# PSUM copies by lateness, dk in 16 B runs, small outputs as rows, K flips on TensorE: a change to a convolution-and-gated-unit gradient kernel

## The chip, the core and the metric

The kernel runs on one core of one Trainium2 chip. The core has five engines with in-order instruction streams of their own: TensorE (PE in the profile, its weight loads PEld), VectorE (DVE), ScalarE (ACT), GpSimd (POOL) and SyncE (SP). Here SP only issues DMAs, and POOL issues most of the others. TensorE writes its results to PSUM, eight banks of 2 KB in each of 128 partitions; VectorE and ScalarE carry them from there to SBUF. The metric is device time in microseconds for one execution that computes all outputs.

## The reference

The forward function takes q, k, v (2048 tokens, 512 channels, bf16) and weights, and the kernel returns its value and nine gradients.

```python
xn = layernorm(q)
k_shift = sum(k shifted by t, t = 0..3, times shift_k[:, t])
kv = k_shift * v
y = irfft(rfft(kv padded) * rfft(ssm_k padded))[:S] + kv * ssm_D
g = silu((sigmoid(xn @ w_gate) * (xn @ w_up)) @ w_down)
out = q + (xn * y) * g
# returned: out, and the gradients of q, k, v, shift_k, ssm_k, ssm_D,
#           w_gate, w_up, w_down for a given grad_out
```

So out_0 is the value, out_1 to out_3 the gradients of q, k and v, out_4 (512 x 4) that of shift_k, out_5 (512 x 2048) that of ssm_k, called dk in the code, out_6 (512) that of ssm_D, and out_7 to out_9 those of the weights.

## The kernel before

**How it is recorded and ordered.** The program isn't written in the order in which it runs. Generators ("streams") call operations on a recorder, `Rec`, which notes each one with its reads and writes. `run_streams` interleaves the streams: each has a weight and a start and end fraction, and the stream that is furthest behind is advanced. That gives every operation a number. At the end `Rec.order` plays all operations through a simple model of the five engines (`cost` for compute, `dcost` for DMAs, whose transfers go through one modelled pipe) and always takes the operation that can start first; equal starts go to the lower number. A PSUM tile gets its banks at that point too, of the kind that it asks for (`mm2`: three pairs of banks; `mm2c`, used in the last stage: two pairs; `acc`: two banks; `tr`: two banks). `emit` then issues the operations in that order, so each engine's in-order stream is fixed by the model's idea of time. All instructions have one source line in the profile, L467, for that reason, and are told apart by engine, operation, shape and place in time.

**Copies out of PSUM.** `evac` (L229) records an operation with two alternatives, a ScalarE copy and a VectorE copy. Before the change both engines have it in their queues of ready work, and the one that can start first takes it. A DMA is held back until it would start at most 8 us ahead of the end of the modelled pipe (L418).

**The stages.** The channels are worked in four column groups of 128 (`cg`).

1. First stage, up to about 160 us. `strK` transposes ssm_k and takes it through `step1` (matmuls with the table Cf) and a flip, a 128 x 128 transposition of blocks from Qg to Qf; `strV` forms kv on VectorE (eight tensor-tensor operations of 2048 elements a group) and does the same; `strX` does `step3`, the complex product `cmul` on VectorE, `inv3` and `inv1`, which leave y. Spectra go to DRAM (KK_d). Beside them `strG` runs the gate and up projections of eight token blocks. V's flips are transposes on TensorE with a PSUM copy (`flip`, L805); K's are two DMA transposes of SBUF (`flip_dma`, L814), issued by SP.
2. The token stage, `stepB`, up to about 395 us: sixteen token blocks through the gated unit and back (z, d, x). Transposed copies of its activations go out through DMA transposes on SP (`token_major`), and are read again as L blocks (`ld_L`) for the weight gradients.
3. The last stage. `frontC` and `backC` take the gradient of y back through the same transform, with KK loaded from DRAM, and `dW` (35 output blocks of 16 matmuls, accumulated in `acc` banks) fills TensorE between them. For each column group `backC` loads vg, ksh and kh (`ld_bwd`, called at L1185 ahead of step3), does four quarters (`qq`) of step3, two products and two inv3, then inv1, forms dks with VectorE and two small SBUF-to-SBUF DMAs for the rows that cross partitions, then makes dk: two PSUM tiles of 16 matmuls with Ci, each copied to dKT (L1225). dKT has the 16 values j of one n side by side, and the copy walks over j outside and n inside. Then follow the diagonal of shift_k (one `tr` bank), seven tensor-tensor operations for the gradient of k, and the stores.

**The end.** After the last group `backC` reorders the diagonals into skout and stores out_4 from it (L1257), and out_6 from dDo (L1258), by SP, both from a layout with channels on partitions: out_4 in pieces of four values, out_6 in pieces of one.

Of the kernel before, what the change touches and what calls it, by code (L numbers as in the profile page):

```python
# [166 lines left out]
class Rec:  # L167
# [141 lines left out]
    def dcost(self, alt):  # L309

        eng, meth, a, k = alt
        dst, src = a[0], a[1]
        nb = math.prod(dst.shape) * esize(dst.dtype)
        if "transpose" in meth:
            return nb / 176e3 + 0.3, nb / 176e3
        run = 1 << 20
        for v in (dst, src):
            dims = [d for d in v.ap if d[1] > 1]
            r = 1
            for s, n in reversed(dims if str(v.space) == "DRAM" else [d for d in v.ap[1:] if d[1] > 1]):  # L320
                if s != r:
                    break
                r *= n
            run = min(run, r * esize(v.dtype))
        rate = 320e3 if run >= 2048 else 280e3 if run >= 1024 else 220e3 if run >= 512 else 120e3 if run >= 256 else run * 400
        par = dst.shape[0] if str(dst.space) != "DRAM" else src.shape[0]
        d = nb / rate
        if par < 16:
            d = min(d * 16, d + 1.0)
        return (0.56 if eng == "gpsimd" else 0.45), d  # L330

    def order(self):
# [23 lines left out]
        now = {e: [] for e in self.ENGS}  # L356
        banks = [0.0] * 8
# [6 lines left out]
        def push(op):  # L364
            for q, alt in enumerate(op.alts):
                heapq.heappush(soon[alt[0]], (op.ready, op.n, q))
# [13 lines left out]
        while ndone < len(ops):  # L380
            best = None
            for e in self.ENGS:
                while soon[e] and (soon[e][0][0] <= free[e] or ops[soon[e][0][1]].done):
                    r, n, q = heapq.heappop(soon[e])
                    if not ops[n].done:
                        heapq.heappush(now[e], (n, q))
                while now[e] and ops[now[e][0][0]].done:
                    heapq.heappop(now[e])
                if now[e]:
                    c = (free[e], now[e][0][0], e, now[e][0][1], True)  # L390
                elif soon[e]:
                    c = (soon[e][0][0], soon[e][0][1], e, soon[e][0][2], False)
                else:
                    continue
                if best is None or c[:2] < best[:2]:
                    best = c
            if best is None:
                raise RuntimeError("the order is stuck: " + str({k: len(v) for k, v in blocked.items()}))
            t, n, e, q, isnow = best
            heapq.heappop(now[e] if isnow else soon[e])  # L400
            op = ops[n]
            new = [v for v in op.tiles if v.bank is None]
# [12 lines left out]
            alt = op.alts[q]  # L415
            if op.dma:
                occ, d = self.dcost(alt)
                t = max(t, pipe - 8.0)  # L418
# [12 lines left out]
            seq.append((op, q, t))  # L431
# [29 lines left out]
    def emit(self):  # L461
        seq = self.order()
        place = lambda v: v.place() if isinstance(v, PT) else v
        with self.tc.manual_schedule(), self.nc.allow_non_contiguous_dma(reason="tiny"):
            for op, q, _ in seq:
# [94 lines left out]
def kernel_impl(ctx, tc, A_q, A_k, A_v, A_shift_k, A_ssm_k, A_ssm_D, B_x, B_w_gate, B_w_up, B_w_down,  # L560
# [296 lines left out]
    def strK():  # L857
        for cg in range(NG):
# [16 lines left out]
            flip_dma(Qg, Qf)  # L875
            yield 1
# [65 lines left out]
    run_streams([(gG, len(FA) * 11776, 0.1, 0.97), (strK(), 4 * 6144, 0.0, 0.7), (strV(), 4 * 16384, 0.0, 0.8),  # L942
# [236 lines left out]
    def backC():  # L1179
        for cg in range(NG):  # L1180
# [4 lines left out]
            ld_bwd(cg)  # L1185
# [4 lines left out]
            for qq in range(5):  # L1190
                if qq < 4:
# [9 lines left out]
                    ys[qq] = (Y1, Y2)  # L1201
                if qq > 0:
# [16 lines left out]
            for jh in range(2):  # L1219
# [5 lines left out]
                nc.evac(dKT[:, :, 8 * jh:8 * jh + 8].rearrange("p n j -> p j n"), pk[:], 1024)  # L1225
# [31 lines left out]
        nc.sync.dma_start(out_4.rearrange("(db p) t -> p db t", p=P), skout)  # L1257
        nc.sync.dma_start(out_6.rearrange("(cg p) -> p cg", p=P), dDo)  # L1258
# [15 lines left out]
    for r in [wdT_r, wgT_r, wuT_r, sig_r, h_r, xq2_r, go_r, dg_r, du_r, wq_r, dh_r,  # L1274
# [17 lines left out]
    term_r = Ring(ar, [NJ, GW])  # L1292
    dm = ar.view(term_r.blks[0][0], [4, 128], f32)
# [4 lines left out]
                        (gated(backC(), "back"), 4 * 38912 + 4096, -0.05, 0.72)], until=lambda: "back" in flags)  # L1298
# [66 lines left out]
```

## Time and profile before

| what | value |
|---|---|
| median of 3 runs | 658.59 us (657.49 to 660.03) |
| the profiled execution | 659.44 us |
| its span, first to last instruction | 657.7 us |
| mean granted TensorE clock | 0.942 |
| DMA, mean over the span | 198 GB/s |
| DMA packets under 512 B | 126311 of 178163 |

The profile shows one execution. The busy time of an engine is the time in which it executes; idle time before an instruction is put down to what it waited for last. In the table by stretches each row gives a stretch, its length and the busy time of PE, PEld, DVE, ACT and POOL with instruction counts, then the granted clock, the mean busy share of the DMA engines and GB/s. A timeline row gives start, length, engine, operation, what it writes and reads, the count of merged instructions, and in brackets the idle time before it with its cause. A row of a group gives busy time and the mean in ns, then the idle time before. A row of DMA issues gives the count, KB each and the median time from issue to landing. SPq is the sequencer of SP.

### The profile page before, as it was taken

What the parts mean: (1) busy time and instruction counts of PE and PEld (TensorE: products, weight loads), DVE (VectorE), ACT (ScalarE), POOL (GpSimd) and SP (SyncE); (2) the same over time, 40 slices, a digit from 0 to 9 for tenths busy, and PEclk for the clock granted to TensorE, in tenths of its full rate; (3) what the DMA queues carried; (4) which work ended last, traced back from release to release, by engine and by line L of the source; (5) the groups of instructions that cost most, each with busy time, mean ns of one, the idle gap of its engine ahead of it and who ended that gap; (6) DMA issues with size and microseconds to landing.
All of it is one profiled execution on the core that took longest, in us unless ns stands there. A gap on an engine that the chain in (4) does not pass through costs nothing.

```text
span 657.7 us, 12345 instructions
## 1 busy us (share of the span) xinstructions
PE 544.7 (83%) x4940; PEld 365.6 (56%) x4996; DVE 489.5 (74%) x921; ACT 286.3 (44%) x352; POOL 150.5 (23%) x259
## 2 busy tenths in 40 slices
PE   4867888997799698998999895599865988998952
PEld 3756667774567465665666562345643554754531
DVE  7599899976889769898887781138627988778704
ACT  7547688641434233443343350114452472552700
POOL 2215143222112222222211020112112133241111
PEclk9979899998899899999999998879977999899996
DMA  8898985999959857998578999999974759585272
GB/s 252 222 225 239 272 222 195 260 224 194 232 146 232 202 137 204 175 225 236 151 186 218 245 242 139 107 253 175 283 201 125 186 170 310 179 273 160 76 57 80
DMA packets 178163, 130.09 MB, mean 198 GB/s; under 512 B 126311, under 2 KB 158905, under 8 KB 178106
## 3 DMA queue, kind: packets, MB, share of 16 engines
q1 hardware_dynamic: 161162, 75.52, 54.0%
q0 software_dynamic: 16416, 53.78, 29.7%
q8 instruction: 39, 0.64, 0.4%
q14 instruction: 18, 0.15, 0.1%
q10 hardware_dynamic: 528, 0.00, 0.0%
HBM read 52.79 MB, written 46.11 MB: 150 GB/s over the span
## 4 chain that ended last, share of the span: by engine, by line
PE 40%; DVE 31%; issue 10%; DMA 10%; ACT 6%; POOL 2%; POOLq 0%; DVEq 0%; ACTq 0%
PE psum L467 40%; DVE slab L467 31%; DMA slab<-slab 7%; ACT slab L467 6%; DMA slab<-in_A_q_dram 2%; POOL slab L467 1%; DMA slab<-in_grad_out_dram 1%; POOL out_dram L467 1%; DMA out_dram<-slab 1%; DVEq L467 0%; POOL KK_d L467 0%; POOLq L1360 0%; POOLq L467 0%; ACTq L467 0%; POOLq L1349 0%
## 5 line engine op out<-in xcount | busy, mean ns | idle before, releaser
L467 PE MATMUL psum<-slab 128*128 128x128 bf16 (+4 forms) x4940 | 544.7, 271 | 101.5 <-DVE slab L467 47.7
L467 PEld LDWEIGHTS <-slab 128*128 128x128 bf16 (+1 forms) x4996 | 365.6, 101 | 280.2 <-issue 87.7
L467 DVE TENSOR_TENSOR slab<-slab 128x512 bf16<-128x512 bf16 (+5 forms) x551 | 301.8, 587 | 30.3 <-DMA slab<-slab 12.8
L467 ACT CAST slab<-psum 128x1024 bf16<-128x1024 f32 (+2 forms) x188 | 179.4, 994 | 209.9 <-PE psum L467 156.1
L467 DVE CAST slab<-psum 128x1024 bf16<-128x1024 f32 (+2 forms) x67 | 73.7, 1108 | 61.0 <-PE psum L467 47.7
L467 POOL DMA_DIRECT2D out_dram<-slab x75 | 44.1, 592 | 275.5 <-DVE slab L467 197.3
L467 ACT ACTIVATE slab<-psum 128x512 bf16<-128x512 f32 (+1 forms) x64 | 36.5, 574 | 55.8 <-PE psum L467 53.3
L467 DVE TENSOR_TENSOR slab<-psum,slab 128x512 bf16<-128x512 f32 (+2 forms) x68 | 44.0, 653 | 19.0 <-PE psum L467 12.7
L467 ACT ACTIVATE slab<-slab 128x512 bf16<-128x512 bf16 (+3 forms) x51 | 40.1, 797 | 40.2 <-DVE slab L467 39.6
L467 ACT COPY slab<-psum 128x512 bf16<-128x512 bf16 (+1 forms) x46 | 34.2, 757 | 48.5 <-PE psum L467 36.4
L467 POOL DMA_DIRECT2D KK_d<-slab x32 | 19.9, 628 | 55.1 <-DVE slab L467 32.2
L467 DVE SCALAR_TENSOR_TENSOR slab<-slab 128x1 f32<-128x1 f32 (+3 forms) x64 | 28.0, 437 | 3.4 <-ACT slab L467 2.2
L467 POOL DMA_DIRECT2D slab<-in_A_q_dram x29 | 16.1, 556 | 50.1 <-ACT slab L467 31.4
L467 DVE SCALAR_TENSOR_TENSOR slab<-psum,slab 128x512 f32<-128x512 f32 x16 | 11.0, 690 | 18.0 <-PE psum L467 18.0
L467 DVE TENSOR_SCALAR slab<-slab 128x1 f32<-128x1 f32 (+8 forms) x49 | 16.8, 358 | 1.7 <-ACT slab L467 1.0
L467 POOL DMA_DIRECT2D slab<-KK_d x16 | 11.6, 728 | 25.3 <-DVE slab L467 25.3
L467 DVE COPY slab<-psum 128x1024 bf16<-128x1024 bf16 (+1 forms) x18 | 11.2, 627 | 4.4 <-PE psum L467 4.1
L467 POOL TENSOR_TENSOR slab<-slab 128x1 f32<-128x1 f32 (+1 forms) x20 | 12.4, 624 | 8.5 <-DVE slab L467 8.3
L467 DVE BATCH_NORM_STATS2 slab<-slab 128x6 f32<-128x512 bf16 x16 | 11.0, 686 | 2.6 <-DMA slab<-in_A_q_dram 2.6
L467 DVE MEMSET slab<- 32x192 uint32 (+2 forms) x7 | 1.1, 165 | 15.2 <-DMA slab<-slab 14.1
L467 POOL DMA_DIRECT2D slab<-in_grad_out_dram x16 | 8.7, 542 | 12.4 <-DMA out_dram<-slab 12.1
L467 POOL DMA_DIRECT2D slab<-in_A_k_dram x12 | 10.1, 845 | 3.9 <-PE psum L467 2.8
(22 smaller groups left out, 43.3 us busy)
## 6 DMA issues: line engine op xcount, KB each, us to landing
KK_d<-slab POOLq DMA_DIRECT2D x32, 256.0 KB, 4.5
slab<-KK_d POOLq DMA_DIRECT2D x16, 512.0 KB, 5.9
out_dram<-slab POOLq DMA_DIRECT2D x58, 128.0 KB, 3.6
hS_d<-slab SPq DMA_DIRECT2D x16, 352.0 KB, 2.9
dgS_d<-slab SPq DMA_DIRECT2D x16, 352.0 KB, 3.5
duS_d<-slab SPq DMA_DIRECT2D x16, 352.0 KB, 3.3
slab<-hS_d SPq DMA_DIRECT2D x8, 512.0 KB, 6.0
slab<-dgS_d SPq DMA_DIRECT2D x8, 512.0 KB, 12.6
```

The costliest lines, as they stand in the source:

```text
L467: getattr(getattr(self.nc, eng), meth)(*[place(v) for v in a], **{x: place(v) for x, v in k.items()})
```

## The change

Five things change in the code, and none in the arithmetic.

1. `order`: an operation with two alternatives is no longer in both engines' queues. ScalarE takes it when it comes first there. VectorE may take it only when ScalarE would start it late: by over 0.4 us if VectorE has nothing else within 0.6 us, by over 1.6 us otherwise.
2. `dcost`: other prices. DMA transposes occupy SP for less time; POOL's DMAs with runs of 256 B or more are priced like runs of 1 KB; other rates are higher; a DMA may now start 9 us ahead of the pipe's end.
3. K flips: `flip` on TensorE instead of `flip_dma`; the weight of `strK` in the interleaving goes from 6144 to 10240 a group. The flips of the last stage (`frontC`) remain DMA transposes.
4. `backC`: the call of `ld_bwd` goes from the start of a group to its third quarter; the copy to dKT walks over n outside and j inside, so that 8 values of 2 B lie side by side in each write; the stream's end fraction goes from 0.72 to 0.66.
5. out_4 and out_6: skout and dDo are multiplied with the identity, which lays their values along the free dimension of four partitions; the result is copied to SBUF and stored as rows.

```diff
@@ dcost
         if "transpose" in meth:
-            return nb / 176e3 + 0.3, nb / 176e3
+            return nb / 260e3, nb / 170e3
...
-        rate = 320e3 if run >= 2048 else 280e3 if run >= 1024 else 220e3 if run >= 512 else 120e3 if run >= 256 else run * 400
+        if eng == "gpsimd" and run >= 256:
+            run = 1024
+        rate = 360e3 if run >= 2048 else 300e3 if run >= 1024 else 250e3 if run >= 512 else 150e3 if run >= 256 else run * 500
...
-        return (0.56 if eng == "gpsimd" else 0.45), d
+        return (0.56 if eng == "gpsimd" else 0.4), d
@@ order
         def push(op):
-            for q, alt in enumerate(op.alts):
-                heapq.heappush(soon[alt[0]], (op.ready, op.n, q))
+            if len(op.alts) > 1:
+                either.append(op)
+            else:
+                heapq.heappush(soon[op.alts[0][0]], (op.ready, op.n))
...
+                if either and e in ("scalar", "vector"):
+                    o = min(either, key=lambda o: (max(o.ready, free[e]), o.n))
+                    s = (max(o.ready, free[e]), o.n, e, 1)
+                    late = free["scalar"] - s[0]
+                    if e == "scalar" or late > (0.4 if c is None or c[0] > s[0] + 0.6 else 1.6):
+                        if c is None or s[:2] < c[:2]:
+                            c = s
...
-                t = max(t, pipe - 8.0)
+                t = max(t, pipe - 9.0)
@@ strK
-            flip_dma(Qg, Qf)
-            yield 1
+            yield from flip(Qg, Qf)
...
-    run_streams([(gG, len(FA) * 11776, 0.1, 0.97), (strK(), 4 * 6144, 0.0, 0.7), (strV(), 4 * 16384, 0.0, 0.8),
+    run_streams([(gG, len(FA) * 11776, 0.1, 0.97), (strK(), 4 * 10240, 0.0, 0.7), (strV(), 4 * 16384, 0.0, 0.8),
@@ backC
             Qf = stC.pop(("Qf", cg))
-            ld_bwd(cg)
...
+                if qq == 2:
+                    ld_bwd(cg)
                 if qq > 0:
                     Y1, Y2 = ys.pop(qq - 1)
...
-                nc.evac(dKT[:, :, 8 * jh:8 * jh + 8].rearrange("p n j -> p j n"), pk[:], 1024)
+                nc.evac(dKT[:, :, 8 * jh:8 * jh + 8], pk[:].rearrange("p j n -> p n j"), 1024)
...
-        nc.sync.dma_start(out_4.rearrange("(db p) t -> p db t", p=P), skout)
-        nc.sync.dma_start(out_6.rearrange("(cg p) -> p cg", p=P), dDo)
+        po = ps_tr([GW, 4], f32)
+        for t in range(4):
+            nc.tensor.matmul(po[0:4, :, t], skout[:, :, t], ident, start=True, stop=True)
+        nc.evac(row4[0:4, :], po[0:4].rearrange("p a t -> p (a t)"), 512)
+        nc.sync.dma_start(out_4.rearrange("(g p) t -> g (p t)", p=P), row4[0:4, :])
+        pd = ps_tr([GW], f32)
+        nc.tensor.matmul(pd[0:4, :], dDo, ident, start=True, stop=True)
+        nc.evac(row6[0:4, :], pd[0:4], 128)
+        nc.sync.dma_start(out_6.rearrange("(g p) -> g p", p=P), row6[0:4, :])
@@ the last stage's streams
-                        (gated(backC(), "back"), 4 * 38912 + 4096, -0.05, 0.72)], until=lambda: "back" in flags)
+                        (gated(backC(), "back"), 4 * 38912 + 4096, -0.05, 0.66)], until=lambda: "back" in flags)
```

33 lines of the change are left out of this document (18 added, 15 removed).

## The prediction

> **What bounds the kernel now.** The page comes first: span, busy times, and the chain that ended last.
>
> ```profile
> span 657.7 us, 12345 instructions
> PE 544.7 (83%) x4940; PEld 365.6 (56%) x4996; DVE 489.5 (74%) x921; ACT 286.3 (44%) x352; POOL 150.5 (23%) x259
> PE 40%; DVE 31%; issue 10%; DMA 10%; ACT 6%; POOL 2%; POOLq 0%; DVEq 0%; ACTq 0%
> ```
>
> No engine is full, and the chain changes hands, so the average settles nothing. The table by stretches does: 40 to 120 is in the first stage (convolution forward), 380 to 440 the border between the token stage and the last one (convolution backward beside the weight gradients), 440 to 620 the last stage, then the tail.
>
> ```profile
> 40.00:120.00 80.00, 66.20 (x746) 52.08 (x754) 76.67 (x112) 59.07 (x68) 25.90 (x42) 0.91 0.88 236
> 380.00:440.00 60.00, 43.20 (x264) 22.28 (x271) 20.51 (x45) 10.90 (x16) 9.17 (x15) 0.86 1.17 186
> 440.00:500.00 60.00, 46.88 (x333) 29.42 (x336) 38.28 (x64) 28.03 (x23) 12.46 (x19) 0.93 0.87 212
> 500.00:620.00 120.00, 109.68 (x738) 65.57 (x751) 97.73 (x137) 55.23 (x45) 32.87 (x51) 0.96 0.62 185
> 620.00:658.00 38.00, 18.99 (x98) 10.05 (x96) 10.99 (x16) 6.19 (x5) 6.07 (x10) 0.79 0.55 86
> ```
>
> The numbers are length, then busy PE, PEld, DVE, ACT, POOL. VectorE fills 76.67 of 80 in the first stage. From 380 TensorE should be the bound, because the weight gradients can fill any hole, yet it is idle 16.8, 13.1, 10.3 and 19.0 us in the four later rows: 59 us. That is the pool from which the change can take. What ends TensorE's waits after 440:
>
> ```profile
> PE psum L467 <- ACT slab L467: 16.4, 6, 7.2
> PE psum L467 <- DVE slab L467: 13.2, 8, 6.2
> ```
>
> **dk copied in 16 B runs.** Here are ScalarE's wide PSUM copies in the whole program, then in 40 to 120, where no dk copy runs, then dk copies of the first, third and fourth column group.
>
> ```profile
> L467 ACT CAST slab<-psum 128x1024 bf16<-128x1024 f32 x115 | 141.7, 1272 | 105.3 <-PE psum L467 91.9 <-DMA slab<-slab 4.1 <-DMA out_dram<-slab 3.0
> L467 ACT CAST slab<-psum 128x1024 bf16<-128x1024 f32 x43 | 42.0, 1016 | 20.8 <-PE psum L467 17.1 <-DMA slab<-slab 3.0 <-ACT slab L467 0.7
> 481.08 4.48 ACT L467 CAST slab<-psum 128x1024 bf16<-128x1024 f32 x1 [1.10 <-PE psum L467]
> L467 ACT CAST slab<-psum 128x1024 bf16<-128x1024 f32 x2 | 9.0, 4718 | 1.5 <-PE psum L467 1.5
> 615.97 8.96 ACT L467 CAST slab<-psum 128x1024 bf16<-128x1024 f32 x2 [1.50 <-PE psum L467]
> 3.29 1.57 ACT L467 CAST slab<-psum 128x512 bf16<-128x512 f32 x3
> ```
>
> A dk copy takes about 4.6 us against 1.02 for its sort; 8 x 3.6 explain the raised mean (115 x 1.272 = 146.3; less 107 x 1.02 = 109.1 leaves 37, 4.65 each). It writes single 2 B elements 32 B apart. After the change it writes runs of 8 (16 B), as step1's copies do, which are among the 43 at 1.016. New is the read: a jump of 512 B in PSUM per element. No row shows that; the nearest is the last one above, the shift-kernel broadcast (L768), which reads every fourth word and takes 1.57/3 = 0.52 us. So a new dk copy lies between 1.02 and 4.65; I take 1.02, from the rows with equal runs.
>
> The Trainium skill (SBUF — State Buffer, "Door 1: The DMA port swizzle") says that SBUF has 16-byte lines, with a penalty for each access that crosses to a new line, and PSUM 8-byte lines. By its first half the old stores pay and the new ones do not, as the 4.65 and the 1.016 show; by its second half the new reads pay 1024 times and the copy stays near the old price. The 0.52 us row, which changes the 8-byte line at every element, speaks against that.
>
> What of the 8 x 3.6 = 29 us is on the path is read from TensorE's stops:
>
> ```profile
> 479.18 3.62 PE L467 MATMUL psum<-slab 128*128 128x128 bf16 x27 [3.39 <-ACT slab L467]
> 485.60 7.30 PE L467 MATMUL psum<-slab 128*128 128x128 bf16 x44 [2.80 <-ACT slab L467]
> 538.82 17.23 PE L467 MATMUL psum<-slab 128*128 128x512 bf16 x95 [0.75 <-ACT slab L467]
> 580.41 23.17 PE L467 MATMUL psum<-slab 128*128 128x512 bf16 x120 [1.22 <-ACT slab L467]
> ```
>
> 3.39 + 2.80 + 0.75 + 1.22 = 8.2; elsewhere weight gradients cover the copy. **-8 us** (-4 if other waits step in, -13 if VectorE's 6.2 us wait, which follows the first group's copies, goes too).
>
> **Small outputs as rows.** The tail, in order:
>
> ```profile
> 617.63 16.83 PE L467 MATMUL psum<-slab 128*128 128x512 bf16 x92 [0.22 <-DVE slab L467]
> 620.80 3.59 SPq L467 DMA_DIRECT2D out_dram<-slab  x2
> 640.82 7.52 DVE L467 TENSOR_TENSOR slab<-slab 128x2048 bf16<-128x2048 bf16 x6 [12.79 <-DMA slab<-slab]
> 641.12 0.81 ACT L467 CAST slab<-psum 128x352 bf16<-128x352 f32 x2 [10.95 <-DMA out_dram<-slab]
> 641.63 4.53 PE L467 MATMUL psum<-slab 128*128 128x352 bf16 x16 [7.17 <-ACT slab L467]
> 648.64 1.68 POOL L467 DMA_DIRECT2D out_dram<-slab  x2 [5.70 <-DVE slab L467]
> out_dram<-slab SPq DMA_DIRECT2D x1, 1.0 KB, 17.5
> out_dram<-slab POOLq DMA_DIRECT2D x4, 1024.0 KB, 7.1
> out_dram<-slab POOLq DMA_DIRECT2D x8, 88.0 KB, 4.8
> ```
>
> The two SP issues at 620.80 are out_6 (2 B runs, 17.5 us to landing) and out_4 (8 B runs). From there nothing lands for some 15 us: VectorE waits 12.79 for the shifted dks rows, ScalarE 10.95 for a free output buffer, TensorE 7.17. As rows they are four runs of 1 KB and four of 256 B. Then TensorE goes on: 617.63 + 16.83 + 4.53 = 639.0; last copy about 0.5, issue 0.54, 88 KB store 4.8: 644.9. The end now lies 2 us after the last landing (648.64 + 7.1 = 655.7, span 657.7), so 646.9: **-11 us**. VectorE's branch stays inside: the rows it waits for are issued 2 x 3.6 us sooner behind the dk copies, the six products need 7.52 and the 1 MB store 7.1, ending about 643. Added: five matmuls, two copies of 0.6, two stores. Behind the matmuls on TensorE stand weight gradients, which wait if VectorE brings skout late: 0 to 2 us. Bounds -7 (TensorE's wait alone) and -13 (VectorE's).
>
> **Copies to VectorE only when ScalarE is behind.** Row of VectorE's wide copies after 440:
>
> ```profile
> L467 DVE CAST slab<-psum 128x1024 bf16<-128x1024 f32 x23 | 28.0, 1223 | 23.1 <-PE psum L467 20.7 <-ACT slab L467 2.3
> ```
>
> These 23 hold 28 us of VectorE and, since it works in order, another 23 us of waiting for matmuls, with complex products queued behind. ScalarE has 180 - 83 = 97 us idle between 440 and 620, and a copy costs it 1.02 for 1.22. TensorE's 13.2 us behind VectorE should shrink by about half: **-6 us** (0 to -10). What is late next is ScalarE's own queue, by up to the 1.6 us that the rule allows.
>
> **K flips on TensorE.** Added: 4 x 32 = 128 transposes and 16 copies. Removed: eight transposes from SP's queue and the engines.
>
> ```profile
> 48.24 1.13 PE psum L467 x16
> L467 ACT COPY slab<-psum 128x1024 bf16<-128x1024 bf16 x10 | 9.9, 1023 | 0.7 <-PE psum L467 0.7
> 63.99 9.37 SPq L467 DMA_TRANSPOSE slab<-slab  x1
> ```
>
> Sixteen such transposes take 1.13: 128 cost TensorE 9.0 us, against 13.8 idle in 40 to 120 and more outside. Sixteen copies at 1.02 are 16.4 us for ScalarE, which has 20.9 idle there; on VectorE, which has 3.3, they would lengthen the stage directly. Against that: SP is held 9.37 us by one such DMA, the first group's spectrum is ready some 15 us sooner, and the copy rule takes a few copies off VectorE. **-1 us**, between -9 and +9.
>
> **The rest.** Moving the loads of vg, ksh and kh to the third quarter changes their number, not their readiness: the planner picks what can start first, and the number breaks ties (L395). POOL has nothing else ready at that point, so I cost it at nothing. The stream share 0.66 for 0.72 also only numbers operations. The new transfer prices shift the order by small amounts everywhere: 0, plus or minus 6.
>
> **Sum.** -8 - 11 - 6 - 1 = -26. The profiled execution took 659.44 us, 1.74 more than its span; 633.4. The median shown, 658.59, lies 0.85 lower: **632.6 us**.
>
> **Rivals.** *The border stall goes too.*
>
> ```profile
> 385.09 43.42 DMA slab<-slab x2
> 409.45 2.29 PE L467 MATMUL psum<-slab 128*128 128x512 bf16 x5 [8.01 <-DVE slab L467]
> 428.55 11.72 PE L467 MATMUL psum<-slab 128*128 128x512 bf16 x40 [7.92 <-DMA slab<-slab]
> slab<-KK_d POOLq DMA_DIRECT2D x2, 512.0 KB, 18.4
> slab<-in_A_v_dram POOLq DMA_DIRECT2D x1, 1024.0 KB, 29.6
> slab<-slab SPq DMA_TRANSPOSE x5, 23.3
> slab<-slab SPq DMA_TRANSPOSE x72, 5.6
> ```
>
> Between 380 and 430 five transposes run among POOL's loads and land in 23.3 us, where all 72 have 5.6; the loads are slow as well, and TensorE loses 8.01 + 7.92. If the moved loads do come later, most of that is saved: 632.6 - 14 = 618.6. Against it: the argument on ties above. 17%.
>
> *The dk copy stays slow*, by its jumping read: the 8 us return and about 3 in the tail, 644. For it: no row has that read. Against it: the 0.52 us row. 10%.
>
> *The tail was not the small stores' doing*, but the 1 MB store's beside them: the change does not do what it says. Only the 7.17 of TensorE's wait and part of the landing return: 641. Against it: stores of that size land in 7.1 us. 8%.
>
> *Slower: loads crowd the transposes.* The planner now prices POOL's 256 B and 512 B runs like 1 KB ones and lets transfers run 9 us ahead, not 8. At the border some 2.5 MB of loads (KK, vg, ksh) beside five transposes cost about 18 us of landing time: 7 us a MB. The kernel gets slower if the four flips of the last stage together meet over 26/7 = 3.7 MB more than now; a group loads up to 2.5 MB, so two groups suffice. With three groups, 7.5 MB: +52 - 26, about 685. Against it: weight gradients cover part, and 500 to 620 shows DMA 0.62 busy. 8%.
>
> *The copies overload the first stage*: +9 there, no gain of 6 after 440, and re-ordering costs 6 and TensorE's filler another 4: 658, no change. 7%.
>
> **Numbers.** Forecast 50%, own range 622 to 643; together with the rivals 100%. The range 606 to 655 takes in the border case, both mis-sized cases and most of the bounds (all gains at their ends: -13 - 13 - 10 - 9 gives 613.6, and part of the border's 14). Half a per cent is 3.3 us, about what a measurement can tell. Faster: 50 + 17 + 10 + 8 = 85%; same 7%; slower 8%.
>
> **What would show it.** dk copies near 1.02 us on ScalarE; no 3.39 and 2.80 stops of TensorE behind ScalarE; no DMA wait over 5 us in the last 40 us, with the last weight gradient ending the span; fewer than 12 wide copies on VectorE after 440; VectorE still above 90% between 40 and 120; a stall of 15 us or more on transposes at the border. I am wrong if the border shrinks, if dk copies stay above 3 us, or if the first stage ends over 9 us later.

## The result, and the profile after

The changed kernel takes 606.37 us (median of 4 runs, 605.38 to 615.58) against 659.31 us beside it (657.49 to 662.66): ratio 0.9187, 95% interval 0.9138 to 0.9235. That is 53 us less where 26 were forecast, at the very edge of the range. The profiled execution took 606.13 us, 1.73 more than its span. Some executions are slower, mostly at a lower granted clock: the ratios leave these out, e3 below has too few others for a ratio, medians of all runs can lie some us above what the ratio says, and the profiles of e1, e2, e3, e6 and e9 are of such executions.

The page, in the same three rows as before: span, busy time of each engine, and the chain that ended last.

```profile
span 604.4 us, 12639 instructions
PE 545.8 (90%) x5129; PEld 371.2 (61%) x5129; DVE 430.7 (71%) x863; ACT 320.8 (53%) x428; POOL 150.9 (25%) x259
PE 42%; DVE 24%; DMA 15%; ACT 8%; issue 8%; POOL 2%; POOLq 0%; DVEq 0%; ACTq 0%
```

TensorE is busy as long as before (545.8 us against 544.7) in 53.3 us less span. Most of the gain is waiting that went. The table by stretches says where (length, then busy PE, PEld, DVE, ACT, POOL, clock, DMA share, GB/s):

```profile
40.00:120.00 80.00, 75.07 (x954) 62.05 (x954) 70.05 (x112) 74.16 (x89) 26.38 (x45) 0.97 0.71 202
380.00:440.00 60.00, 55.30 (x356) 29.97 (x353) 27.50 (x58) 24.03 (x30) 13.78 (x21) 0.97 1.04 231
440.00:500.00 60.00, 54.40 (x416) 33.58 (x415) 44.28 (x73) 32.79 (x37) 20.46 (x30) 0.99 0.85 234
500.00:560.00 60.00, 59.28 (x407) 36.02 (x406) 43.73 (x68) 30.41 (x37) 15.80 (x25) 0.99 0.90 239
560.00:604.00 44.00, 37.59 (x241) 20.42 (x238) 12.67 (x16) 10.88 (x17) 9.55 (x16) 1.00 0.42 125
```

From 380 on TensorE is idle 4.7 + 5.6 + 0.7 + 6.4 = 17 us, where it was idle 59: 42 us less. What still ends its waits there (releaser, sum, count, longest):

```profile
PE psum L479 <- DMA slab<-slab: 6.5, 2, 3.5
PE psum L479 <- ACT slab L479: 3.2, 5, 2.1
PE psum L479 <- DVE slab L479: 2.6, 3, 1.4
```

ScalarE's 16.4 and VectorE's 13.2 have gone to 3.2 and 2.6, and so have the two stops of 8 us at the border. The wide copies after 420, by engine, and three neighbours in the timeline; the second and third are dk copies of the last group:

```profile
L479 ACT CAST slab<-psum 128x1024 bf16<-128x1024 f32 x72 | 71.5, 1017 | 53.7 <-PE psum L479 47.8 <-DVE slab L479 2.9 <-DMA out_dram<-slab 2.8
L479 DVE CAST slab<-psum 128x1024 bf16<-128x1024 f32 x3 | 3.7, 1225 | 24.6 <-PE psum L479 24.0 <-issue 0.6
```

```profile
562.24 1.01 ACT L479 CAST slab<-psum 128x1024 bf16<-128x1024 f32 x1 [0.34 <-PE psum L479]
563.83 1.01 ACT L479 CAST slab<-psum 128x1024 bf16<-128x1024 f32 x1 [0.58 <-PE psum L479]
565.53 1.01 ACT L479 CAST slab<-psum 128x1024 bf16<-128x1024 f32 x1 [0.69 <-PE psum L479]
```

A dk copy now costs what every other wide copy costs, and VectorE has 3 wide copies left of 23. The tail:

```profile
575.23 7.52 DVE L479 TENSOR_TENSOR slab<-slab 128x2048 bf16<-128x2048 bf16 x6 [0.52 <-DMA slab<-slab]
582.89 16.08 PE L479 MATMUL psum<-slab 128*4 128x128 bf16 x95 [1.38 <-DVE slab L479]
599.05 0.45 ACT L479 CAST slab<-psum 128x352 bf16<-128x352 f32 x1 [1.93 <-PE psum L479]
599.79 0.54 POOL L479 DMA_DIRECT2D out_dram<-slab  x1 [1.84 <-ACT slab L479]
```

The six products no longer wait 12.79 us for the shifted rows, TensorE runs on, and its last weight gradient ends the span.

To compare the runs, the last stage is cut at five points that are the same instruction in every kernel: the end of the x step of token block 14 (called x14 below), then the first step3 copy of each column group in `backC`, then the end. Times are from the profiled executions, in us.

| kernel | x14 at | to group 0 (the border) | to group 1 | to group 2 | to group 3 | to the end | last stage |
|---|---|---|---|---|---|---|---|
| before | 393.8 | 47.4 | 27.2 | 52.9 | 57.3 | 79.1 | 263.9 |
| changed | 388.8 | 31.6 | 28.9 | 41.3 | 43.8 | 70.0 | 215.6 |

Up to x14 the change gives 5 us, which is less than one kernel varies there: its repeat e9 below reaches x14 at 398.6. Behind x14 it gives 48.3, 15.8 of these at the border, which the prediction had left as it was, and 32.5 in the four parts behind the border (216.5 to 184.0). The last stage as one stretch, before and after:

```profile
393.80:657.70 263.90, 205.26 (x1315) 118.86 (x1334) 156.54 (x234) 93.47 (x77) 56.33 (x87) 0.91 0.77 173
388.80:604.40 215.60, 197.76 (x1344) 114.95 (x1342) 122.04 (x199) 94.73 (x114) 56.41 (x87) 0.98 0.81 213
```

TensorE is idle 17.8 us there for 58.6, and it is busy 7.5 us less, at a granted clock of 0.98 for 0.91. So some 7 us of the gain are shorter busy time and not waits; they go with the higher clock, and no run changes the clock alone.

### The profile page after: what moved, and what is told of

Read it like the earlier page. It is cut to its first block, busy times and chain, and to the rows that moved or that the text cites. A ratio compares the mean times of both kernels' runs of the same rounds, so it can differ in the third digit from the quotient of the medians.

```text
span 604.4 us, 12639 instructions
## 1 busy us (share of the span) xinstructions
PE 545.8 (90%) x5129; PEld 371.2 (61%) x5129; DVE 430.7 (71%) x863; ACT 320.8 (53%) x428; POOL 150.9 (25%) x259
## 4 chain that ended last, share of the span: by engine, by line
PE 42%; DVE 24%; DMA 15%; ACT 8%; issue 8%; POOL 2%; POOLq 0%; DVEq 0%; ACTq 0%
PE psum L479 42%; DVE slab L479 24%; ACT slab L479 8%; DMA slab<-slab 8%; DMA KK_d<-slab 3%; DMA slab<-in_grad_out_dram 2%; DMA out_dram<-slab 1%; POOL out_dram L479 1%; POOL slab L479 1%; DMA slab<-in_A_k_dram 1%; POOL KK_d L479 0%; POOLq L1381 0%; DVEq L479 0%; POOL sF_d L479 0%; POOL hF_d L479 0%
## 5 line engine op out<-in xcount | busy, mean ns | idle before, releaser
L479 PE MATMUL psum<-slab 128*128 128x128 bf16 (+5 forms) x5129 | 545.8, 269 | 53.2 <-ACT slab L479 26.1
L479 PEld LDWEIGHTS <-slab 128*128 128x128 bf16 (+2 forms) x5129 | 371.2, 100 | 227.4 <-issue 42.6
L479 ACT CAST slab<-psum 128x1024 bf16<-128x1024 f32 (+4 forms) x245 | 201.5, 855 | 176.5 <-PE psum L479 143.4
L479 POOL DMA_DIRECT2D out_dram<-slab x75 | 44.2, 592 | 220.2 <-DVE slab L479 138.1
L479 ACT COPY slab<-psum 128x1024 bf16<-128x1024 bf16 (+1 forms) x65 | 53.1, 830 | 28.2 <-PE psum L479 27.9
L479 DVE CAST slab<-psum 128x1024 bf16<-128x1024 f32 (+1 forms) x12 | 14.1, 1178 | 30.7 <-PE psum L479 27.2
L479 POOL DMA_DIRECT2D KK_d<-slab x32 | 20.3, 639 | 55.8 <-ACT slab L479 41.7
L479 DVE SCALAR_TENSOR_TENSOR slab<-psum,slab 128x512 f32<-128x512 f32 x16 | 11.0, 689 | 18.1 <-PE psum L479 18.1
L479 POOL DMA_DIRECT2D slab<-slab x8 | 4.6, 574 | 27.1 <-DVE slab L479 26.3
(22 smaller groups left out, 39.9 us busy)
```

What stands on the lines that cost most here:

```text
L479: getattr(getattr(self.nc, eng), meth)(*[place(v) for v in a], **{x: place(v) for x, v in k.items()})
```

## The experiments

### One part taken out of the changed kernel

Six kernels put one part back as it was in the kernel before.

```diff
e1: dcost, and "pipe - 8.0", as before
e2: order's queues for operations with two alternatives, as before
e3: -  nc.evac(dKT[:, :, 8 * jh:8 * jh + 8], pk[:].rearrange("p j n -> p n j"), 1024)
    +  nc.evac(dKT[:, :, 8 * jh:8 * jh + 8].rearrange("p n j -> p j n"), pk[:], 1024)
e4: out_4 and out_6 stored straight from skout and dDo, as before
e5: ld_bwd(cg) at the group's start, share 0.72, as before
e6: -  yield from flip(Qg, Qf)
    +  flip_dma(Qg, Qf)
```

> The changed kernel with the old transfer prices and the old 8 us window; all else as changed. Theory P (the 27 us that the prediction missed come from the order that the new prices give, above all at the border and in the last stage): about 630 us, 20 to 30 above the changed kernel, with steps of over 10 us on transposes between 375 and 440. Theory Q (the prediction's own four terms were each too small, the prices are worth nothing): within 6 us of the changed kernel's 606.

> The changed kernel with the old choice of engine for PSUM copies (whichever can start first). The prediction's term: 6 us above the changed kernel, 612, with 20 or more wide copies on VectorE in the last stage. Theory Q: 15 us or more, over 620. Theory P: 606 to 612.

> The changed kernel with dk copied in single 2 B elements again. Its order of instructions is the same. The prediction's term: 8 us above the changed kernel, 614, eight copies near 4.6 us. If the copies lie under TensorE's fill: 606 to 609. Theory Q: over 620.

> The changed kernel with the two small outputs stored as before in 2 B and 8 B pieces. The prediction's term: 11 us above the changed kernel, 617, with all stores issued after them landing over 10 us late. If backC now ends early enough for weight gradients to be loaded and computed meanwhile: 606 to 612. Theory Q: over 620.

> The changed kernel with the loads of vg, ksh and kh called at the start of a group again and the share 0.72. By the prediction's argument (the number only breaks ties): within 4 us of the changed kernel's 606, border as in the changed kernel (step3 of the first group about 32 us after the end of block 14's x step). If the move is what dissolved the border stall: 615 to 625 and step3 about 45 us after.

> The changed kernel with K's flips by DMA transpose again. The prediction's term: within 2 us of the changed kernel, bounds -9 and +9. The changed kernel's first stages are 5 us shorter than before's up to the border (388.8 against 393.8 for the end of block 14's x step); if the flips give those, 611 to 613 here, with the difference all ahead of the border.

| run | median us (range) | ratio to before, 95% | border | to 1 | to 2 | to 3 | to end | last stage |
|---|---|---|---|---|---|---|---|---|
| e1, no new prices | 626.69 (620.94 to 630.44) | 0.9571 (0.9425 to 0.9718) | 45.6 | 26.6 | 42.7 | 33.6 | 79.9 | 228.4 |
| e2, no copy rule | 616.67 (616.04 to 627.78) | 0.9438 (0.9295 to 0.9582) | 43.2 | 22.5 | 40.6 | 49.6 | 68.5 | 224.4 |
| e3, 2 B dk copies | 637.21 (624.09 to 644.83) | none | 28.2 | 28.3 | 55.8 | 41.5 | 76.8 | 230.6 |
| e4, no rows | 617.13 (610.26 to 621.31) | 0.9419 (0.9281 to 0.9558) | 33.5 | 29.7 | 43.1 | 44.2 | 75.0 | 225.5 |
| e5, no load move | 611.58 (607.94 to 619.56) | 0.9222 (0.916 to 0.9284) | 40.5 | 26.8 | 43.2 | 46.8 | 63.4 | 220.7 |
| e6, K flips by DMA | 606.31 (601.01 to 620.38) | 0.9111 (0.9051 to 0.917) | 45.6 | 29.3 | 42.3 | 42.6 | 70.0 | 229.8 |

e1 came out as theory P has it (627 for 630), with the long border; the lowest time of e3 is over 620, as only theory Q has it. Over the last stage, against 215.6: prices 12.8, rule 8.8, dk 15.0, rows 9.9. But these are not the parts' own worth. The border is short (28 to 34) in the changed kernel, e3 and e4, and long (40 to 46) in e1, e2, e5 and e6; and e5 gives its instructions in the same order as the changed kernel up to the middle of the last stage, so that its border differs without a difference of order. So the border has to be taken apart from the rest.

Behind the border the changed kernel takes 184.0 us and its repeat e9 181.7; differences of 2 to 3 us there mean nothing. e1 takes 182.8, e2 181.2 and e5 180.2: without the prices, the rule or the load move nothing is lost behind the border, and what they cost over the last stage lies at the border. e3 takes 202.4, so dk is worth 18.4 there, 14.5 more between groups 1 and 2, 6.8 more in the last part and 2.9 less in the other two. e4 takes 192.0, so the rows are worth 8.0 at most; 5.0 of it stands in the last part, where the outputs are, and the rest in parts whose order e4 shares with the changed kernel. The last part takes 69.9 to 70.1 in the changed kernel, e9, f2 and f5 (the last two below), so the 5.0 is clear.

Without the rows the small stores are back in the tail of e4; its waits from 570 on (who waits, for what, sum, count, longest):

```profile
ACT slab L478 <- DMA out_dram<-slab: 14.7, 2, 9.3
DVE slab L478 <- DMA slab<-slab: 11.2, 1, 11.2
```

The longest, 9.3 and 11.2, are the 10.95 and 12.79 of before: the small stores are their cause, since nothing else in the code was put back. TensorE itself waits 5.4 us there, about what the last part grows by.

### Loads kept from among the transposes

In e7 (on the kernel before) and e8 (on the changed one) the planner may place the first group's vg, ksh and kh loads only behind both flips of that group.

```diff
+        if cg == 0:
+            for op in nc.ops[n0:]:
+                op.deps.update(x.n for x in FLIPS[-2:])
```

> The kernel before, with one thing more: for the first column group the planner may place the loads of vg, ksh and kh only after both flips. Theory C (at the border the transposes crawl because those 2 MB of loads run among them): transposes there land in under 17 us each, step3 of the first group starts 10 to 18 us sooner (30 to 37 us after block 14's x step, not 47), total 643 to 650. Theory O (the stall has another cause and the changed order avoids it otherwise): step3 within 4 us of 47, total within 5 us of before.

> The changed kernel with the same restriction. Theory C: the rest of its border stall (transposes of 16, 16 and 10 us) shrinks as well, 3 to 8 us under the changed kernel, 598 to 603. If those loads went through ahead of the transposes anyway: 604 to 608.

e7 took 645.38 us (637.97 to 650.04; ratio 0.9734, 0.9657 to 0.9812), border 23.2 instead of 47.4, last stage 251.7. e8 took 612.25 us (609.01 to 616.35; ratio 0.9273, 0.9213 to 0.9334), border 25.3, last stage 214.8. So the loads beside the transposes are what makes the border long. In e8 the border gives 6.3 us, the later loads cost 14.0 at group 1 (42.9 for 28.9), 8.7 come back at group 2 (32.6 for 41.3), and the time does not gain.

### Parts alone, and controls

e9 is the changed kernel unaltered, e10 the kernel before with the new prices, e11 the kernel before with the 16 B dk copies, e12 is e6 again.

> The changed kernel once more, unaltered, as the measure for the three runs beside it. Time expected 606 (604 to 612). What is open is the border: in the first profile of the changed kernel the first step3 copy came 31.6 us after the x step of the last token block, in the run without the moved load call, whose instruction order is the same up to there, 40.5 us. Theory A, the border's length is set by the order: again 30 to 34 us and no transpose over 20 us. Theory B, it varies from execution to execution: any value between 28 and 45, and the total moves with it by less than half of that, as weight gradients fill in.

> The kernel before with the new transfer prices and the 9 us alone. Prediction's term: 0, plus or minus 6, so 653 to 665. Theory A, the parts add (taking the prices out of the changed kernel cost 12.8 us in the last stage): 644 to 649, with the last stage (end of the last x step to the end) near 251 instead of 264. Theory B, the prices pay only beside the new copy rule and the fast dk copy, since before them TensorE waits for ScalarE and VectorE there in any order: 654 to 661.

> The kernel before with the 16 B dk copies alone. Prediction's term: -8, between -4 and -13, so 651 (646 to 655), with dk copies near 1.01 us on ScalarE and TensorE's stops of 3.39 and 2.80 us behind ScalarE gone. Theory A, the parts add (taking dk out cost 15 us in the last stage): 643 to 646. Theory B, before the rule and the prices other waits step into the place of the dk copies: 653 to 658. With the order of instructions nearly as before, the tail should still hold its wait of 12 us behind the small stores.

> The changed kernel with K's flips as DMA transposes, once more, since its first profile fell into a disturbed execution though two of its times were the shortest of all, 601.0 and 602.4. Theory A, the flips on TensorE cost what they save: same as the changed kernel beside it, within 3 us. Theory B, they cost TensorE 9 us of transposes and ScalarE 16 us of copies in a stage where both are over 88% busy, and the flips by DMA are hidden: 4 to 5 us faster than the changed kernel beside it. Theory C, they save, as the first profile's last stage (229.8 us against 215.6) would have it: 5 us slower or more.

| run | median us (range) | ratio to before, 95% | border | to 1 | to 2 | to 3 | to end | last stage |
|---|---|---|---|---|---|---|---|---|
| e9, changed again | 611.49 (603.97 to 615.07) | 0.9167 (0.907 to 0.9265) | 32.7 | 26.5 | 41.3 | 43.9 | 70.0 | 214.4 |
| e10, prices alone | 638.08 (632.88 to 641.07) | 0.9643 (0.9561 to 0.9726) | 31.9 | 22.5 | 57.8 | 41.9 | 82.6 | 236.7 |
| e11, dk alone | 648.8 (644.44 to 659.0) | 0.9792 (0.9707 to 0.9876) | 43.6 | 26.8 | 43.2 | 56.6 | 77.7 | 247.9 |
| e12, K flips by DMA | 609.66 (604.3 to 612.01) | 0.9207 (0.9119 to 0.9295) | 33.6 | 30.3 | 43.0 | 44.3 | 70.1 | 221.3 |

The prices alone are worth 3.6% (2.7 to 4.4), and their border is short: of 27.2 us over the last stage 15.5 lie at the border. dk, the only other part that was tried alone, is worth 2.1% (1.2 to 2.9), some 14 us. Of the 16.0 us by which e11's last stage is shorter, 3.8 lie at the border, ahead of any dk copy, and 9.7 between groups 1 and 2, where the dk copies of the first group are. K flips on TensorE make no difference that these runs can tell: e12 and e9 overlap widely. The waits of TensorE in e11, from the first step3 copy to the end, against 16.4 and 13.2 in the kernel before:

```profile
PE psum L467 <- ACT slab L467: 14.7, 3, 7.2
PE psum L467 <- DVE slab L467: 5.0, 3, 3.3
```

The two stops of 3.39 and 2.80 behind ScalarE are gone, and so is VectorE's 6.19; ScalarE's 7.2 of the tail stays, as do the small stores that cause it. ScalarE's sum falls by only 1.7, because a new stop of 6.91 has come near the place of the old ones. How the slow copies reached VectorE, and what is new, stands in the timelines, first before, then e11:

```profile
491.40 0.69 DVE L467 TENSOR_TENSOR slab<-psum,slab 128x512 f32<-128x512 f32 x1 [7.52 <-PE psum L467]
501.40 2.29 PE L467 MATMUL psum<-slab 128*128 128x256 bf16 x9 [6.19 <-DVE slab L467]
```

```profile
481.70 0.69 DVE L467 TENSOR_TENSOR slab<-psum,slab 128x512 f32<-128x512 f32 x1 [2.73 <-PE psum L467]
489.05 1.01 ACT L467 CAST slab<-psum 128x1024 bf16<-128x1024 f32 x1 [6.12 <-DMA slab<-slab]
490.11 42.58 PE L467 MATMUL psum<-slab 128*128 128x256 bf16 x285 [6.91 <-ACT slab L467]
```

VectorE's row is the diagonal of shift_k. It waits for the matmuls that TensorE issues behind the dk copies, and it comes 23.0 us after the first step3 copy of group 1 before, 13.8 us in e11. Behind it VectorE works in order through its products, and then comes a PSUM copy (at 500.13 before, 490.42 in e11) for which TensorE waited the 6.19 us. The new stop is a copy on ScalarE that waited 6.12 us for a DMA transpose.

### The border: one instruction moved

In the kernels so far SP issues, around x14, a store of a token-major copy (dgS_d, 352 KB), an L-block load, and two DMA transposes; the second transpose writes into the buffer that this store reads, so it can't go out before the store has landed. The store, the two transposes and POOL's load of vg at the border of the kernel before, in the timeline:

```profile
381.14 1.20 SPq L467 DMA_DIRECT2D dgS_d<-slab  x1
385.09 4.39 SPq L467 DMA_TRANSPOSE slab<-slab  x1
389.59 15.45 SPq L467 DMA_TRANSPOSE slab<-slab  x1
391.83 1.16 POOL L467 DMA_DIRECT2D slab<-in_A_v_dram  x1 [5.05 <-issue]
```

and of the changed one:

```profile
377.60 0.63 SPq L479 DMA_DIRECT2D dgS_d<-slab  x1
380.15 4.91 SPq L479 DMA_TRANSPOSE slab<-slab  x1
386.82 1.16 POOL L479 DMA_DIRECT2D slab<-in_A_v_dram  x1 [4.98 <-issue]
388.34 10.22 SPq L479 DMA_TRANSPOSE slab<-slab  x1
```

Before, the store has landed at 388.7, the first transpose holds SP until 389.48, and the second goes out right then, 2.2 us ahead of the 1 MB load of vg. In the changed kernel, whose new prices put the store behind the L-block load, SP is free at 385.06, but the store lands only at 388.3, and the second transpose goes out then, 1.5 us after the load. The load itself goes out 2.0 us ahead of x14 in every run but e7 and e8. f1 and f2 test this race by moving that store in the emitted order and nothing else.

```diff
f1, kernel before: the store goes from ahead of the L-block load
    and the first transpose to right behind that transpose
f2, changed kernel: the store goes from right behind the L-block load to ahead of it
```

> The kernel before, with one SP instruction moved and nothing else: the second store of a token-major copy at the border goes from ahead of an L-block load and the first of the pair of transposes to right behind that transpose. Theory A, a race decides the border: the second transpose goes out when that store has landed; where it goes out before the 1 MB load of vg (2.0 us ahead of the end of block 14's x step in every run) both crawl and land 22 to 29 us after that end, where it goes out later the load lands at 12 to 18 and the transpose at 15 to 20. Then here: transpose behind the load, the load landed 12 to 18 us after that end, the first step3 copy 29 to 36 us after it (47.4 in the first profile, 43.6 in the run with dk alone), and the time 4 to 10 us shorter, 649 to 656. Theory B, the order of that pair only goes with something else: copy at 43 to 47 us, time 657 to 662.

> The changed kernel, with one SP instruction moved the other way: the same store goes from behind the L-block load to ahead of it, as in the kernel before. Theory A: the store lands some 5 us sooner, the second transpose goes out ahead of the 1 MB load, that load lands 22 to 29 us after the end of block 14's x step instead of 12 to 14, the first step3 copy comes 40 to 46 us after it instead of 32, and the time is 3 to 8 us longer, 608 to 615. Theory B: copy at 30 to 34 us, time 604 to 608.

f1 took 642.78 us (641.12 to 644.06; ratio 0.9773, 0.9688 to 0.9858), f2 615.7 us (613.15 to 625.38; ratio 0.9351, 0.9257 to 0.9445).

| kernel | x14 at | border | to 1 | to 2 | to 3 | to end | last stage |
|---|---|---|---|---|---|---|---|
| f1, before with the store later | 395.2 | 29.3 | 26.5 | 52.7 | 57.3 | 80.3 | 246.1 |
| f2, changed with the store sooner | 389.5 | 39.9 | 27.3 | 41.4 | 43.2 | 70.1 | 221.9 |

f1 differs from the kernel before at the border, by 18.1 us, and nowhere else in the last stage by over 1.2; f2 from the changed one at the border, by 8.3 us, and nowhere else by over 1.6. The order of one store is the cause of the long border. The DMA view says how it comes: GB/s in forty slices of the stretch that begins with the first transpose (385 to 424 in the kernel before, 386 to 410 in f1), and in the second row the load's time to landing. First the kernel before, then f1:

```profile
GB/s 411 400 371 276 76 71 79 85 142 125 134 85 102 97 82 85 207 205 196 61 192 204 166 166 178 100 112 128 128 93 93 60 112 50 29 39 33 85 80 75
...
slab<-in_A_v_dram POOLq DMA_DIRECT2D x1, 1024.0 KB, 29.6
```

```profile
GB/s 394 407 375 335 271 172 108 192 64 90 81 67 81 43 122 37 58 121 100 103 136 336 352 408 402 392 361 335 328 330 364 335 253 140 255 92 35 57 291 454
...
slab<-in_A_v_dram POOLq DMA_DIRECT2D x1, 1024.0 KB, 13.8
```

Each starts near 400 GB/s and falls below 200, at times below 50, when a transpose and loads are in flight together. In f1 the rate is back at 336 in the 22nd slice, about 399, some 3 us before the first transpose has landed, and stays between 328 and 408 for eleven slices. In the kernel before the second transpose is out by then and the crawl lasts to the end. f2 against the changed kernel is the same, 23.9 us against 14.4:

```profile
slab<-in_A_v_dram POOLq DMA_DIRECT2D x1, 1024.0 KB, 23.9
```

```profile
slab<-in_A_v_dram POOLq DMA_DIRECT2D x1, 1024.0 KB, 14.4
```

All 18 profiled executions other than e7 and e8 fall in line. In eight (before, e1, e2, e5, e6, e11, f2, f4) the second transpose goes out 2.0 to 6.7 us ahead of x14, with or ahead of the load, and the load lands 22 to 28 us after x14; in ten it goes out between 0.5 ahead and 10.0 after, and the load lands 8 to 17 after. In the changed order it is close: in e2, e5 and e6 the store landed 1.5 to 1.8 us sooner than in the changed kernel's profile and the transpose came level with the load, which fits that e5 crawled with an unchanged order. The Trainium skill (DMA: Bandwidth & Descriptors, "Queues, rings and completion order") says that each DMA engine takes turns between the queues that have work, a packet at a time. That fits a load that is slowed by a transpose beside it; it does not say why the order of the second transpose and the load decides between 29.6 and 13.8. The number of transposes in flight alone does not do it: in the changed kernel both are in flight beside the load from 0.5 us ahead of x14 to 7.6 after it, and the load takes 14.4. Why the rate falls so low, and why the order counts, is not settled here.

### Which of the prices

f3 is the kernel before with the line of rates alone, f4 with all other new prices but not that line.

```diff
f3: -  rate = 320e3 if run >= 2048 else 280e3 if run >= 1024 else ...
    +  rate = 360e3 if run >= 2048 else 300e3 if run >= 1024 else ...
f4: the transposes' price, POOL's runs, 0.4 for 0.45, 9 us for 8
```

> The kernel before with the line of DMA rates alone (360, 300, 250, 150 and run x 500 for 320, 280, 220, 120 and run x 400). Theory A, the prices' 20 us alone come from the planner believing the pipe free sooner, which is what the rates say: most of it here, 638 to 645, with the store behind the L-block load at the border and the first step3 copy at 29 to 36 us. Theory B, it takes the transposes' price, POOL's runs or the 9 us as well: 650 to 660.

> The kernel before with the other new prices (transposes, POOL's runs, SP's 0.4, 9 us ahead) and the old line of rates. Theory A: little of the 20 us, 652 to 662, the store ahead of the load at the border as before and the first step3 copy at 40 to 47 us. Theory B: 638 to 648.

f3 took 653.34 us (646.45 to 662.19; ratio 1.0008, 0.9916 to 1.0099), f4 668.94 us (663.2 to 669.91; ratio 1.0172, 1.0088 to 1.0257). The place was right and the total wrong. In f3 the store is behind the load and the border 33.4; its last stage has 237.9 us, as e10's 236.7. In f4 the store is ahead, the border 44.1, the last stage 254.7. So the rates alone bring the last stage's gain, but not the kernel's: f3 reached x14 at 415.8 and f4 at 406.7, later than the kernel before by 22 and 13. TensorE's waits behind VectorE up to the end of `strX`, in the kernel before, in f3 and in f4:

```profile
PE psum L467 <- DVE slab L467: 18.1, 17, 4.5
```

```profile
PE psum L467 <- DVE slab L467: 26.2, 13, 7.3
```

```profile
PE psum L469 <- DVE slab L469: 31.1, 17, 7.0
```

They are 8 and 13 us longer, so a part of the loss stands in the first stage. The granted clock up to x14 is lower too, 0.93 in f3 and 0.94 in f4 for 0.97 before. The prices together reach x14 at 402.2 (e10). How much of it belongs to the order and how much to the execution is open: e3 and e9, whose order up to there is that of the changed kernel, reached x14 at 401.2 and 398.6 against 388.8.

### The race taken out

f5 moves the store in the changed kernel to right behind the first transpose; f6 does the same with K's flips as DMA transposes.

> The changed kernel, with the same store moved once more, from ahead of the first transpose of the pair to right behind it, so that the second transpose cannot go out before the 1 MB load. Theory A, the race decides the border and is open in the changed kernel (the store lands 0.2 to 2.4 us around the load's issue): the border is short in every execution, the profiled last stage 208 to 217 us (215.6 in the first profile), the times lie closer together and their median at 600 to 606. Theory B, the race is won anyway in the changed kernel: 604 to 608, no difference. If the pair of transposes is now the late one, its second lands after 20 us and the time is 608 to 614.

> The same move of the store, in the changed kernel with K's flips as DMA transposes. If the flips on TensorE cost what they save: the same time as the run beside it within 3 us. If they cost TensorE and ScalarE more than they save: 3 to 6 us less than it, 596 to 602. If they save: 3 us more or worse.

f5 took 603.67 us (596.35 to 610.39; ratio 0.9178, 0.9092 to 0.9264), f6 600.38 us (594.86 to 607.85; ratio 0.9146, 0.9068 to 0.9224). Their profiled spans are 594.5 and 594.4, and the load and the transposes of f5:

```profile
slab<-in_A_v_dram POOLq DMA_DIRECT2D x1, 1024.0 KB, 10.3
...
slab<-slab SPq DMA_TRANSPOSE x3, 7.8
```

In f5 the parts are 25.0, 27.2, 41.4, 43.2 and 69.9, last stage 206.7: again only the border differs from f2 and the changed kernel by over 1.7. In the profile f5 is the shortest together with f6, 10 us below the changed kernel; f6 has the lowest median of all. By the ratios, whose intervals overlap with the changed kernel's, a gain over it is not shown. That the times would lie closer together, as theory A had it, did not come: 596 to 610.

## Why the prediction was wrong

The sign was right, the size half of what came, and the failed step is **the rest**, "The new transfer prices shift the order by small amounts everywhere: 0, plus or minus 6". They are worth 3.6% alone (e10), 27.2 us over the last stage, and 15.5 of these stand at the border, where one store that they put behind one load decides (17.8 for that store alone in f1). Out of the changed kernel they cost 12.8 us there (e1), none of it behind the border. A planner that fixes the order of five engines turns a small price into a swap, and a swap can decide a race. The working had looked at the moved call for a reason that the border might go, found rightly that it gives none, and stopped there.

- **The border stall.** The mechanism was seen: five transposes among POOL's loads. Its price was near: 14 us against f1's 18 in the last stage. The condition was wrong. "If the moved loads do come later" did not happen, as argued: vg goes out 2.0 us ahead of x14 in both kernels. A stall of 15 us or more on transposes was named as a sign of being right; TensorE's waits behind them are 6.5 in sum. Nothing comes from the moved call: e5 costs 5.1 us over the last stage, less than the 6.3 of f2, which has the same long border, and is not slower behind the border. What would have shown it: the second transpose at 389.59 and the load at 391.83 were in the trace, 2.2 us apart, and the store for which that transpose has to wait had landed only 0.9 us before it. The sign named beforehand ("I am wrong if the border shrinks") is the one that came.
- **dk copies.** Duration right, 1.01 us for 1.02. The term was mis-sized: -8 forecast, with -13 "if VectorE's 6.2 us wait, which follows the first group's copies, goes too". It went too: behind the border dk is worth 12.2 us alone (e11), inside these bounds, and 18.4 last (e3), beyond them. The stops charged to ScalarE, 8.2, were not all that the slow copies cost. The two copies of a group delay the matmuls of the diagonal, and with them VectorE's products and its next PSUM copy, and the wait for that stood under VectorE's name; in the tail another 6.8 us came free once the small stores no longer held it (1.4 in e11, with the small stores).
- **Small outputs as rows.** The mechanism is right, with the same waits back in the same place in e4. The size is less than forecast: for -11, with bounds -7 and -13, e4 shows 5.0 in the last part and 8.0 at most behind the border. No DMA wait over 5 us is left in the last 40 us, and the last weight gradient ends the span, as said.
- **Copies to VectorE only when ScalarE is behind.** 3 wide copies are left where fewer than 12 were expected (17 in e2, without the rule). The 6 us do not show in the last stage: e2's 8.8 is its long border, and behind the border it takes 181.2 us, where f2 takes 182.0 and the changed kernel 184.0. The 13.2 us behind VectorE, half of which was booked here, go to 5.0 with dk alone (e11), so they were for the larger part the dk copies' doing.
- **K flips on TensorE.** -1 forecast; f5 and f6 have the same span within 0.1 us. That VectorE would stay above 90% in 40 to 120 was a miss: 70.05 of 80, while ScalarE rose from 59.07 to 74.16.
- **Slower.** Of the jams that POOL's lower prices might make at the four flips none came: the parts up to groups 2 and 3 are 41.3 and 43.8 for 52.9 and 57.3. The 2.5 MB that the working gives for a group is what is loaded at the border; four KK of 512 KB, ksh, kh and, for every second group, vg make 3 to 4 MB for a whole one.

The sum by what was measured in the last stage: of the 48.3 us, 15.8 lie at the border, which the prediction priced at nothing in its sum, and 32.5 behind it, where it had booked 25 for dk, rows and rule. There dk makes 18.4 (e3) and the rows 5.0 to 8.0 (e4), and prices, rule and load move nothing that shows (e1, e2, e5). So it is luck that 25 lies as near to 32.5 as it does: dk was set too low, rows and rule too high. Each is what its part is worth when the others are there. In the kernel before, the prices alone save 11.7 behind the border (e10), so what a part saves depends on which others are there, and no run here splits the missing 6 to 9 us further.

The weighing of the Trainium skill (SBUF — State Buffer, "Door 1: The DMA port swizzle") came out as the row of the shift kernel had it. e3 writes 2 B at a time again; its wide copies from the first step3 copy to the end:

```profile
L478 ACT CAST slab<-psum 128x1024 bf16<-128x1024 f32 x72 | 99.3, 1427 | 49.4 <-PE psum L478 47.8 <-DVE slab L478 1.1 <-ACT slab L478 0.3
```

That is 27.8 us more than the changed kernel's 71.5 for as many, 3.5 for each of the eight dk copies, as the 16-byte lines of SBUF would have it. The 8-byte lines of PSUM do not show in a ScalarE copy: a read that jumps 512 B at each element costs 1.01 us, as one in sequence does. The page itself speaks of matmuls there.

## What to carry to other kernels

Where a planner fixes the order, a change of its prices is a change of the kernel: compare the two orders at the places where queues meet, and look for pairs of instructions on different queues that stand within a few us and whose order decides what is in flight together. A slow copy can cost more than the stops that carry its name: here 12 to 18 us for 8.2, since VectorE's work behind it was late as well. Results that are laid out across partitions in pieces of 2 or 8 B can be worth a matmul with the identity before they are stored, at the end of a kernel above all; here it was 5 us.

## What was unexpected in the hardware

One 352 KB store issued some 6 us later, with nothing else touched, made the same kernel 18 us shorter over its last stage (f1): a 1 MB load that went out behind a second DMA transpose took 29.6 us, and 13.8 where that transpose came after it. In the changed kernel, e9, f2 and f5, which have the same order behind the border, the parts to groups 2 and 3 and to the end repeat within 0.7 us, though their borders differ by up to 14.9. The border of the same order took 28.2 us (e3), 31.6, 32.7, 33.5 (e4) and, in e5, 40.5.
